# A two-layer squared-ReLU MLP: the first chunk's first layer split into two token halves

## The chip, the cores and the metric

The kernel runs on one core of one Trainium2 chip. Times are device microseconds (us) of a whole execution. A time is about 1.8 us longer than the span that the profile covers (118.68 against 116.9 us in the profiled run). Each timed run also records the mean clock that TensorE was granted. Runs of one kernel are called slow when they are over 1.5% above its fastest run, and the verdicts compare fast runs only. The recorded clock is either 0.999 to 1.0, or 0.985 and, twice, 0.971. I say "full clock" and "dipped" for the two, and compare full-clock runs with full-clock runs.

## The reference

```python
B, S, D, F = 1, 2048, 640, 1536            # all tensors bf16
h = jnp.einsum("bsd,df->bsf", x, w1) + b1
r = jnp.where(h > 0, h, 0)
out = jnp.einsum("bsf,fd->bsd", r * r, w2) + b2
```

## The kernel before

The 2048 tokens are taken in 4 chunks of 512. The first layer makes h with F on the partitions, in 12 F-blocks of 128; each F-block is a sum over KD = 5 blocks of the D dimension. ScalarE (ACT) applies bias and ReLU from PSUM, VectorE (DVE) squares, and the second layer multiplies with w2, 128 tokens by 320 output columns at a time. A layer of one chunk is about 13 us of TensorE time.

The opening is special. Chunk 0 of x is loaded row by row in two halves of 256 tokens and transposed on TensorE. The five D-blocks of w1 arrive one after the other, so the loads are on the clock. The kernel works in rows: one row takes one D-block `k` of w1, for one token half, over the first six F-blocks, which sit in six PSUM banks of 512 columns.

```python
def pass_matmul(j, k, half, last):          # one F-block j, one D-block k, 256 tokens
    reqs = [(s_w1k[k], 16), (s_xT, half * KD + k + 1)]
    ...
    pe.matmul(banks[bname][:, half * HC:(half + 1) * HC],
              lhsT=w1_sb[:, k, j * P:(j + 1) * P], rhs=xT[:, k, half * HC:(half + 1) * HC],
              start=(k == 0 and half == 0), stop=(k == KD - 1), ...)

def pass_row(k, half):
    for j in range(NPASS):                  # NPASS = 6 of the 12 F-blocks
        pass_matmul(j, k, half, False)

dummy(NDUM0)                                # 7 throw-away matmuls while x loads
...                                         # transposes of token half 0
pass_row(0, 0)
pass_row(1, 0)
t_unit(1, 0, ...); t_unit(1, 1, ...)        # transposes of token half 1
pass_row(2, 0)
...                                         # further rows of both halves, k = 4 last
for j in range(NPASS, KF):                  # the other six F-blocks, all 512 tokens
    for k in range(KD):
        mm1_matmul(j, k, ...)
...                                         # then the second layer of chunk 0
```

The loads are issued in this order: x half 0, w1 blocks 0 and 1, x half 1, w1 block 2, b1, w1 blocks 3 and 4, b2, w2.

## Time and profile before

| before | |
|---|---|
| median of the first 4 runs | 117.76 us (116.51 to 118.68) |
| span of the profiled run | 116.9 us |
| TensorE busy | 111.9 us, 96% of the span |
| first matmul of the second layer (in the chain) | 23.56 us |

From the page of the kernel before come the busy times of the engines and two groups: line, engine, operation, out from in, count, busy us and mean ns of one, then idle us before them and what ended it.

```profile
PE 111.9 (96%) x694; PEld 68.0 (58%) x694; DVE 38.7 (33%) x91; ACT 33.8 (29%) x51; POOL 0.7 (1%) x6
L282 PE MATMUL o_ps<-w_sb,r2T 128*128 128x320 bf16 (+1 forms) x396 | 52.8, 295 | 0.0
L245 PE MATMUL h_ps<-xT,w_sb 128*128 128x256 bf16 x30 | 6.0, 323 | 1.8 <-DMA w_sb<-in_w_dram 1.8
```

The whole of TensorE's waiting for data is in line 245, the rows of the opening: 1.8 us for w1. The chain of waits of the same run (start us, us, what) shows how much of the program an opening can move:

```profile
2.69 6.74 DMA w_sb<-in_w_dram
9.42 0.05 issue
9.47 0.82 PE h_ps L245 x3
...
22.48 1.08 PE o_ps L263 x5
23.56 13.04 PE o_ps L282 x96
36.60 12.95 PE h_ps L263 x60
```

The chain runs through the load of the third w1 block, then through TensorE with no further wait. After 23.56 us come pieces of 13.04 and 12.95 us in turn, 96 and 60 matmuls one after the other without a wait. So the date of the first second-layer matmul decides the time. The timeline of TensorE (start us, us, engine, line, operation; in brackets the idle time before and what ended it) shows the two waits, and something else:

```profile
7.65 0.50 PE L245 MATMUL h_ps<-xT,w_sb 128*128 128x256 bf16 x3 [1.30 <-DMA w_sb<-in_w_dram]
9.47 0.82 PE L245 MATMUL h_ps<-xT,w_sb 128*128 128x256 bf16 x3 [0.50 <-DMA w_sb<-in_w_dram]
11.15 0.85 PE L245 MATMUL h_ps<-xT,w_sb 128*128 128x256 bf16 x3
14.31 0.49 PE L245 MATMUL h_ps<-xT,w_sb 128*128 128x256 bf16 x3
```

Three matmuls take 0.50 us at 7.65, over 0.8 us at 9.47 and 11.15, and 0.49 us again at 14.31. The windows view (stretch, its length, then busy us and count of PE, PEld, DVE, ACT and POOL, the granted clock PEclk, DMA share, GB/s) gives the reason:

```profile
6.13:9.54 3.41, 1.50 (x13) 0.82 (x12) 0.49 (x2) 0.00 (x0) 0.00 (x0) 0.99 1.00 356
9.54:12.96 3.42, 3.42 (x20) 2.61 (x21) 0.58 (x3) 0.00 (x0) 0.00 (x0) 0.51 0.86 292
12.96:16.37 3.41, 3.41 (x32) 2.87 (x31) 0.22 (x1) 0.52 (x2) 0.00 (x0) 1.00 0.95 347
```

In a stretch in which TensorE was busy 1.50 of 3.41 us, the clock was still full; in the next stretch of the same length it was halved. The clock records of this trace begin at about 6.1 us: full for 3.413 us, half for 3.413 us, then full for 105.813 us, which is 31.0 times 3.413; in the trace of the changed kernel the full clock lasts 109.226 us, 32.0 times 3.413. So I take stretches of 3.41 us, counted from the first record, as the windows to look at. That the work in one window decides the clock of the next is my reading of the traces. Here the window before the dip was not wholly idle, it was 44% busy. The dip lasts 3.41 us and, at a granted clock of 0.51, costs, by my estimate, about half of that, 1.7 us, of work.

### The profile page before, as it was taken

To read this page: it belongs to the slowest core of one execution; us is meant where nothing else is said; L and a number is where in the kernel's file an instruction comes from. 1 tells how busy PE (TensorE), PEld (TensorE's weight loads), DVE (VectorE), ACT (ScalarE), POOL (GpSimd) and SP (SyncE) were. 2 spreads that over 40 slices of the span, in tenths; PEclk is the share of its full clock that TensorE was granted. 3 is DMA by queue.
4 is the path that set the end of the run, shared out by engine and by line. 5 is a ranking of instruction groups with operands and counts; after the bars stand their busy time and mean duration, and the time that the engine had idled before them with its cause. 6 is when DMAs were issued, how large, how long until landed. Compare 5 with 4: busy or idle time off the path is not lost.

```text
span 116.9 us, 1659 instructions
## 1 busy us (share of the span) xinstructions
PE 111.9 (96%) x694; PEld 68.0 (58%) x694; DVE 38.7 (33%) x91; ACT 33.8 (29%) x51; POOL 0.7 (1%) x6
## 2 busy tenths in 40 slices
PE   7958999999999999999999999999999999999992
PEld 2525784477775444477775444577775444577781
DVE  0303027543323334433322433433332343342331
ACT  5000059720000676520001567610002656700000
POOL 2000000000000000000000000000000000000000
PEclk9996799999999999999999999999999999999999
DMA  3998962701110390001110370001111000001112
GB/s 86 319 340 301 370 217 54 171 0 56 56 41 21 87 193 0 0 0 59 59 59 34 86 161 3 0 0 62 56 56 56 0 0 0 6 0 56 56 56 56
DMA packets 13359, 9.44 MB, mean 81 GB/s; under 512 B 8488, under 2 KB 12712, under 8 KB 13352
## 3 DMA queue, kind: packets, MB, share of 16 engines
q1 hardware_dynamic: 13352, 9.34, 26.4%
q8 instruction: 5, 0.08, 0.3%
q14 instruction: 2, 0.02, 0.0%
HBM read 4.75 MB, written 2.62 MB: 63 GB/s over the span
## 4 chain that ended last, share of the span: by engine, by line
PE 90%; DMA 6%; SPq 1%; issue 0%; DVE 0%
PE o_ps L282 45%; PE h_ps L263 36%; DMA w_sb<-in_w_dram 6%; PE h_ps L245 3%; PE o_ps L245 3%; PE e_ps L263 2%; PE o_ps L263 1%; PE e_ps L233 1%; SPq L181 0%; SPq L182 0%; SPq L184 0%; SPq L183 0%; DVE o_sb L381 0%; PE e_ps L313 0%
## 5 line engine op out<-in xcount | busy, mean ns | idle before, releaser
L282 PE MATMUL o_ps<-w_sb,r2T 128*128 128x320 bf16 (+1 forms) x396 | 52.8, 295 | 0.0
L282 PEld LDWEIGHTS o_ps<-w_sb,r2T 128*128 128x128 bf16 x396 | 38.1, 98 | 14.9
L351 ACT ACTIVATE r_sb<-h_ps,b1T 128x512 bf16<-128x512 f32 x42 | 28.7, 689 | 55.8 <-PE h_ps L263 53.6
L263 PE MATMUL h_ps<-xT,w_sb 128*128 128x512 bf16 x195 | 42.7, 379 | 0.0
L263 PEld LDWEIGHTS h_ps<-xT,w_sb 128*128 128x128 bf16 x195 | 19.1, 98 | 22.5
L372 DVE TENSOR_TENSOR r2T<-r_sb 128x512 bf16<-128x512 bf16 x48 | 20.4, 425 | 32.0 <-ACT r_sb L351 32.0
L381 DVE TENSOR_TENSOR o_sb<-o_ps,b_bc 128x320 bf16<-128x320 f32 (+1 forms) x33 | 15.9, 481 | 33.5 <-PE o_ps L282 33.5
L245 PE MATMUL h_ps<-xT,w_sb 128*128 128x256 bf16 x30 | 6.0, 323 | 1.8 <-DMA w_sb<-in_w_dram 1.8
L245 PE MATMUL o_ps<-xT,w_sb 128*128 128x256 bf16 x30 | 5.7, 312 | 0.0
L245 PEld LDWEIGHTS h_ps<-xT,w_sb 128*128 128x128 bf16 x30 | 3.0, 114 | 2.8 <-DMA w_sb<-in_w_dram 2.3
L365 DVE COPY xT<-e_ps 128x256 bf16<-128x256 bf16 x7 | 1.8, 290 | 6.4 <-PE e_ps L233 6.4
L227 PE MATMUL o_ps<-const-bfloat16-1.0 128*128 128x512 bf16 x7 | 3.1, 624 | 0.8 <-PEq L410 0.8
L245 PEld LDWEIGHTS o_ps<-xT,w_sb 128*128 128x128 bf16 x30 | 3.4, 114 | 0.8
L343 ACT ACTIVATE b1T<-e_ps 128x12 f32<-128x12 bf16 x1 | 0.2, 181 | 11.5 <-PE e_ps L313 11.5
L351 ACT ACTIVATE r_sb<-o_ps,b1T 128x512 bf16<-128x512 f32 x4 | 2.5, 702 | 0.4 <-PE o_ps L263 0.4
L263 PE MATMUL e_ps<-xT,w_sb 128*128 128x512 bf16 x10 | 2.3, 379 | 0.0
L233 PE MATMUL e_ps<-ident,x_sb 128*128 128x128 bf16 x14 | 2.1, 286 | 0.1
L365 DVE COPY xT<-h_ps 128x256 bf16<-128x256 bf16 x3 | 0.7, 292 | 4.4 <-PE h_ps L233 4.4
L227 PEld LDWEIGHTS o_ps<-const-bfloat16-1.0 128*128 128x128 bf16 x7 | 0.9, 135 | 2.1 <-issue 2.1
L233 PEld LDWEIGHTS e_ps<-ident,x_sb 128*128 128x128 bf16 x14 | 1.5, 135 | 0.6 <-issue 0.4
L263 PEld LDWEIGHTS e_ps<-xT,w_sb 128*128 128x128 bf16 x10 | 1.0, 98 | 1.0
L342 ACT ACT_TABLE_LOAD x1 | 1.3, 1283 | 0.7 <-PEq L410 0.7
(14 smaller groups left out, 5.8 us busy)
## 6 DMA issues: line engine op xcount, KB each, us to landing
out_dram<-o_sb SPq DMA_DIRECT2D x15, 160.0 KB, 1.8
w_sb<-in_w_dram SPq DMA_DIRECT2D x5, 384.0 KB, 6.7
w_sb<-in_w_dram SPq DMA_DIRECT2D x1, 1920.0 KB, 12.4
x_sb<-in_x_dram SPq DMA_DIRECT2D x2, 320.0 KB, 4.7
b_bc<-in_b_dram SPq DMA_DIRECT2D x1, 160.0 KB, 7.4
out_dram<-o_sb SPq DMA_DIRECT2D x1, 80.0 KB, 1.6
out_dram<-o_sb SPq DMA_DIRECT2D x2, 40.0 KB, 1.5
xT<-in_x_dram SPq DMA_TRANSPOSE x3, 4.8
```

What stands on the lines that cost most here:

```text
L227: pe.matmul(banks["o0"], lhsT=ones_w, rhs=ones_m, start=True, stop=True)
L233: ins = pw.emit(reqs if q == 0 else [], lambda: pe.transpose(out=stage[(half, k)][:, q * P:(q + 1) * P], in_=x_sb[:, t, k * P:(k + 1) * P] ...
L245: ins = pw.emit(reqs, lambda: pe.matmul(banks[bname][:, half * HC:(half + 1) * HC], lhsT=w1_sb[:, k, j * P:(j + 1) * P], rhs=xT[:, k, half ...
L263: ins = pw.emit(reqs, lambda: pe.matmul(banks[bname], lhsT=w1_sb[:, k, j * P:(j + 1) * P], rhs=xT[:, k, c * CH:(c + 1) * CH], start=(k == ...
L282: ins = pw.emit(reqs, lambda: pe.matmul(banks[bname][:, 0:nc_], lhsT=r2T[:, j, i * P:(i + 1) * P], rhs=w2_sb[:, j, c0:c0 + nc_], start=(j ...
L342: act.activation(out=junk[:, 0:1], in_=zero_c, func=ACT.Relu)
L343: aw.emit([(s_b1ps, 1)], lambda: act.activation(out=b1T[:], in_=e_ps[:, 1, 0:KF], func=ACT.Identity)).then_inc(s_b1T, 1)
L351: aw.emit(reqs, lambda: act.activation(out=r_sb[:, n % NR, :], in_=banks[g1_bank[n]], func=ACT.Relu, bias=b1T[:, j:j + 1], scale=1.0,)).th ...
L365: dw.emit([(s_T, u + 1)], lambda: dve.tensor_copy(out=xT[:, k, half * HC:(half + 1) * HC], in_=stage[(half, k)],)).then_inc(s_xT, 1)
L372: dw.emit([(s_r, n + 1)], lambda: dve.tensor_tensor(out=r2T[:, j, c * CH:(c + 1) * CH], in0=r_sb[:, n % NR, :], in1=r_sb[:, n % NR, :], op ...
L381: dw.emit([(s_b2, 16), (s_o, m + 1)], lambda: dve.tensor_tensor(out=o_sb[:, i, c0:c0 + nc_], in0=banks[g2_bank[m]][:, 0:nc_], in1=b2_bc[:, ...
```

## The change

The intent: do the first layer of chunk 0 for one token half over all 12 F-blocks, then for the other half, so that work downstream (activation, square, second layer of the first 256 tokens) can start earlier.

```diff
-    x_v = x2.rearrange("(i p) d -> p i d", p=P)
+    x_v0 = x2[0:CH, :].rearrange("(p t) d -> p t d", t=TPC)     # 4 neighbouring tokens per partition
+    out_v0 = out2[0:CH, :].rearrange("(p t) d -> p t d", t=TPC)
...
+        for half in range(2):
+            for j in range(KF):
+                q = j // 2                                      # two F-blocks share one bank
+                bname = (pass_banks if half == 0 else b0_banks)[q]
+                G1.append(dict(..., tok0=half * HC, ntok=HC, bank=bname, col0=(j % 2) * HC, ...))
...
-                    reqs = [(s_r2, c * KF + j + 1)]
+                    reqs = [(s_r2, n_of(i, j) + 1)]             # only the half that holds token tile i
...
-            def pass_row(k, half):
-                for j in range(NPASS):
-                    pass_matmul(j, k, half, False)
+            def pass_row(k):
+                for j in range(KF):                             # 12 F-blocks instead of 6
+                    half_matmul(G1[j], k, j % 2 == 0, [])
...
-            pass_row(0, 0)
-            pass_row(1, 0)
+            pass_row(0)
+            pass_row(1)
...                                                             # rows 2 and 3, k = 4, then all of half 1
```

A PSUM bank (a part of 512 columns of the kernel's `psum_tensor` buffers, in which it adds up the five D-blocks of a sum) that held one F-block of 512 tokens now holds two F-blocks of 256 tokens, and only the first of the two starts with `start=True`. All eight experiment runs of kernels built that way are recorded as correct; no run here starts both, so what a second start would do is not shown. The cost of the change is 12 more ACT and 12 more DVE operations, each half as wide, and 120 matmuls of 256 columns where there were 60 of 256 and 30 of 512.

## The prediction

> **What bounds the kernel now.** The page's busy table gives the TensorE 111.9 us of a 116.9 us span (96%), and the chain of waits is 90% TensorE. From 23.56 us on (first second-layer matmul) the chain is TensorE with no gap: alternating pieces of 13.04 and 12.95 us, then 13.09 and a short tail. The change does not touch those 93.3 us. So only the time until the first second-layer matmul can move.
>
> In that opening the timeline shows TensorE waiting 1.3 us for the second block of w1 (6.34 to 7.65 us), and 0.5 us for the third (to 9.47). The rows before use only 6 of the 12 F-blocks per arriving w1 block, so TensorE runs dry. From the issue times and times to landing, I put the fourth and fifth blocks at about 10.5 and 11.4 us, w2 at about 18.2 us. From 9.54 to about 12.95 us the window view gives a granted clock of 0.50: there a 256-column matmul takes 0.213 us instead of 0.109. [...] It costs about 1.7 us, and would explain that the four times fall into 116.5 and 117.0 against 118.6 and 118.7: with or without it.
>
> **What the change does.** Same multiplications: 60 matmuls of 256 plus 30 of 512 columns become 120 of 256. Measured spacing 0.109 against 0.216 us, so +0.06 us. Weight loads are 98 ns and stay hidden. But each arriving w1 block now feeds 12 matmuls at once, so 12 more (1.3 us) are done by the time the third block lands. ACT and DVE get 24 half-size operations instead of 12 in the first chunk: the 512-column ones come every 0.58 us; I estimate 0.36 us for half size, so ACT lags TensorE by up to 3 us but ends near 22 us; the first second-layer groups (6.5 us) need only the first token half, so this is hidden. The x loads get 2560-byte runs: 1280-byte packets take 61 ns, 3072-byte ones 141, so hardly a gain.
>
> **Critical path after** (estimate, full clock): second w1 block 7.65; 12 matmuls 1.31; transposes 0.4; third row 1.31; transposes 0.4; fourth 1.31; 0.3; fifth 1.31; second half 60 x 0.109 = 6.54: second-layer start at about 20.5 us. With full clock I work out 21.85 for the kernel before; so the gain is 1.3 us in like states. The earlier start of downstream work itself gives nothing beyond that: TensorE was already continuous there.
>
> The shorter idle (0.8 us instead of 1.3, plus little) may also avoid the half-clock window; I give this 60 to 65%. Times: the time exceeds the span by 1.8 us, so 20.5 + 93.3 + 1.8 = 115.6 without, 117.3 with a half-clock stretch.
>
> **Predicted:** 115.7 us, range 114.5 to 117.3. Against the fast runs of before (116.7) that is about 1% faster, so the verdict is most likely within 2%: 0.75; faster by over 2%: 0.21; slower: 0.04.
>
> **Right if:** wait for the second block about 0.8 us, for the third under 0.2; second-layer pieces still 13.0 us each; second-layer start at 20.5 us (22.2 with a half-clock stretch); no TensorE wait on ACT or DVE. **Wrong if:** TensorE waits for r2 or a bank at the second layer's start (ACT slower per half than 0.36 us); w1 blocks land later or in another order; the half-clock stretch appears at another place; the 256-column matmuls run at more than 0.11 us.

## The result and the profile after

The changed kernel takes 115.27 us (median of 11 runs, 114.67 to 115.63) against 116.84 us (16 runs, 116.14 to 118.68). The ratio is 0.987, with a 95% interval of 0.984 to 0.990. It is the mean time of the one kernel's fast runs over that of the other's from the same rounds, so not quite the ratio of these medians. By the interval it is a gain of 1.3%. The outputs are right.

From the page of the changed kernel, the engines and the two groups (line 303 was 282, line 267 was 245):

```profile
PE 109.4 (96%) x724; PEld 70.0 (62%) x724; DVE 40.6 (36%) x103; ACT 35.3 (31%) x63; POOL 0.7 (1%) x6
L303 PE MATMUL o_ps<-w_sb,r2T 128*128 128x320 bf16 (+1 forms) x396 | 52.8, 295 | 0.0
L267 PE MATMUL h_ps<-xT,w_sb 128*128 128x256 bf16 x60 | 7.5, 273 | 0.5 <-DMA w_sb<-in_w_dram 0.5
```

The second layer costs what it cost, ACT and DVE gained 1.5 and 1.9 us that nobody waits for, and the rows wait 0.5 us for w1 instead of 1.8. The mean of 273 against 323 ns is the missing half clock: in a trace of the kernel before without it (below) the same group has 273 too. The chain of waits:

```profile
2.59 6.63 DMA w_sb<-in_w_dram
9.22 0.04 issue
9.27 0.83 PE h_ps L267 x6
...
19.38 1.09 PE o_ps L267 x10
20.47 13.04 PE o_ps L303 x96
33.51 12.95 PE h_ps L286 x60
```

The second layer starts at 20.47 us instead of 23.56, and from there on the pieces are the same 13.04 and 12.95 us. The span fell from 116.9 to 113.8 us: the whole difference lies before the second layer. But the profile of before was a dipped run and this one is not, so of these 3.1 us about 1.7 belong to the dip. The waits of TensorE in the changed kernel (who waited for whom: us in total, times, longest) hold a surprise:

```profile
PE e_ps L255 <- DMA x_sb<-in_x_dram: 0.8, 1, 0.8
PE h_ps L267 <- DMA w_sb<-in_w_dram: 0.5, 1, 0.5
```

I had expected 0.8 us of waiting for the second w1 block. It had landed at 5.9 us in this run, so row 1 followed row 0 at once; the 0.8 us went to the second half of x, whose transposes stand next in TensorE's order, and 0.5 us to the third block. Either way TensorE goes on to run dry until the third block, whose row starts at 9.47 us in the first trace and at 9.27 in this one. That block is the gate, and the useful question is how much was done before it opens.

### The profile page after: what moved, and what is told of

Same layout as the page of the kernel before. It is cut to its first block, busy times and chain, and to the rows that moved or that the text cites. A ratio compares the mean times of both kernels' runs of the same rounds, so it can differ in the third digit from the quotient of the medians.

```text
span 113.8 us, 1746 instructions
## 1 busy us (share of the span) xinstructions
PE 109.4 (96%) x724; PEld 70.0 (62%) x724; DVE 40.6 (36%) x103; ACT 35.3 (31%) x63; POOL 0.7 (1%) x6
## 4 chain that ended last, share of the span: by engine, by line
PE 90%; DMA 6%; SPq 1%; DVE 0%; issue 0%
PE o_ps L303 46%; PE h_ps L286 34%; DMA w_sb<-in_w_dram 6%; PE h_ps L267 5%; PE o_ps L267 3%; PE e_ps L267 2%; SPq L206 0%; SPq L205 0%; SPq L204 0%; SPq L203 0%; PE e_ps L255 0%; DVE o_sb L399 0%; PE e_ps L332 0%
## 5 line engine op out<-in xcount | busy, mean ns | idle before, releaser
L369 ACT ACTIVATE r_sb<-h_ps,b1T 128x512 bf16<-128x512 f32 (+1 forms) x48 | 29.5, 652 | 52.8 <-PE h_ps L286 52.7
L286 PE MATMUL h_ps<-xT,w_sb 128*128 128x512 bf16 x180 | 39.3, 379 | 0.0
L390 DVE TENSOR_TENSOR r2T<-r_sb 128x512 bf16<-128x512 bf16 (+1 forms) x60 | 22.3, 372 | 27.8 <-ACT r_sb L369 26.1
L286 PEld LDWEIGHTS h_ps<-xT,w_sb 128*128 128x128 bf16 x180 | 17.6, 98 | 20.7
L267 PE MATMUL h_ps<-xT,w_sb 128*128 128x256 bf16 x60 | 7.5, 273 | 0.5 <-DMA w_sb<-in_w_dram 0.5
L267 PEld LDWEIGHTS h_ps<-xT,w_sb 128*128 128x128 bf16 x60 | 5.6, 98 | 1.3 <-DMA w_sb<-in_w_dram 0.7
L267 PEld LDWEIGHTS o_ps<-xT,w_sb 128*128 128x128 bf16 x40 | 3.9, 98 | 0.5
L369 ACT ACTIVATE r_sb<-o_ps,b1T 128x256 bf16<-128x256 f32 x8 | 3.3, 558 | 0.0
L267 PE MATMUL e_ps<-xT,w_sb 128*128 128x256 bf16 x20 | 2.3, 272 | 0.0
L267 PEld LDWEIGHTS e_ps<-xT,w_sb 128*128 128x128 bf16 x20 | 2.0, 98 | 0.2
L369 ACT ACTIVATE r_sb<-e_ps,b1T 128x256 bf16<-128x256 f32 x4 | 1.7, 571 | 0.0
```

The source lines that it names most:

```text
L267: return pw.emit(reqs, lambda: pe.matmul(g1_view(g), lhsT=w1_sb[:, k, j * P:(j + 1) * P], rhs=xT[:, k, g["tok0"]:g["tok0"] + HC], start=(k ...
L286: ins = pw.emit(reqs, lambda: pe.matmul(g1_view(g), lhsT=w1_sb[:, k, j * P:(j + 1) * P], rhs=xT[:, k, g["tok0"]:g["tok0"] + CH], start=(k ...
L369: aw.emit(reqs, lambda: act.activation(out=r_sb[:, n % NR, 0:g["ntok"]], in_=g1_view(g), func=ACT.Relu, bias=b1T[:, j:j + 1], scale=1.0,)) ...
L390: dw.emit([(s_r, n + 1)], lambda: dve.tensor_tensor(out=r2T[:, j, g["tok0"]:g["tok0"] + g["ntok"]], in0=r_sb[:, n % NR, 0:g["ntok"]], in1= ...
```

## The experiments

All ratios are to fast runs of the kernel before of the same chip, taken beside it. By the 1.5% rule a dipped run can still be called fast; for the token order alone, the rows of 6 and the wait for both halves, which ran on one chip, three of the five fast runs of before were dipped, so there the full-clock means and the traces count for more than the ratio. The theory: in the wait for the loads, rows of 12 F-blocks do 12 matmuls more (1.3 us) before the third w1 block than rows of 6; and because TensorE idles less, the dip disappears. Rivals: the larger x packets bring the loads in earlier; the earlier start downstream is the gain; the runs with a dip have some other cause.

### The kernel before, at full clock

No edit; one look.

> The kernel before, unchanged, once more for its profile. If the run has no half-clock stretch: span about 115 us, second-layer start near 21.85 us (my arithmetic in the prediction, never seen in a trace). If it has one: 23.5 us as before. When the second w1 block lands is the open point: 7.65 us in the first trace of before, 5.93 us in the trace of the changed kernel.

This run took 116.52 us at a clock of 1.0, with a span of 114.7 us. Its chain of waits:

```profile
2.69 6.21 DMA w_sb<-in_w_dram
8.90 0.05 issue
8.95 0.50 PE h_ps L245 x3
...
21.39 13.04 PE o_ps L282 x96
```

Without a dip the kernel before starts its second layer at 21.39 us; I had worked out 21.85. The third w1 block came 0.5 us earlier here than in the first trace, and that is nearly the whole difference. So the fair measure is the distance from the gate to the second layer: 21.39 - 8.95 = 12.44 us before, and 20.47 - 9.27 = 11.20 us after. The gain by this measure is 1.24 us. I use the distance below, as it takes the luck of the loads out.

This trace also suggests why only some runs of one kernel dip. Its windows view, with the windows laid where the trace's clock records put them:

```profile
3.77:7.18 3.41, 1.88 (x20) 1.29 (x20) 1.08 (x5) 0.00 (x0) 0.00 (x0) 1.00 0.93 303
7.18:10.60 3.42, 2.63 (x28) 2.06 (x26) 0.98 (x4) 0.00 (x0) 0.00 (x0) 1.00 0.89 344
```

In the dipped trace the full clock came only at about 6.1 us (three matmuls of its first row still took 0.85 us), so that both waits for w1, 1.30 and 0.50 us, fell into one window, 1.50 us busy. Here it came at 3.77 us, the waits were shared between two windows, 1.88 and 2.63 us busy, and the clock stayed full. So in these traces a window with 1.50 us of work in 3.41 was followed by half the clock and one with 1.88 was not, and where the windows fall differs from run to run: the full clock began at about 6.1, at 3.77 and, in the trace of the changed kernel, at about 4.7 us. This is read from traces; no run here sets where they fall.

### The token order alone

```diff
  (kernel before)
-            sp.dma_start(out=x_sb[:, 0:2, :], in_=x_v[:, 0:2, :])
+            sp.dma_start(out=x_sb[:, 0:2, :], in_=x_v0[:, 0:2, :])
   (and the same for the second half of x and the first four output tiles)
```

> The kernel before with only the change's token order (x and the first outputs four rows apart, 2560-byte x runs). Theory (wider rows fill the wait): no gain, ratio 0.997 to 1.003 to before, because the third w1 block still gates. Rival (the larger x packets let the weights land earlier, and that is the gain): ratio about 0.987, and every w1 block lands over 1 us earlier.

Measured: 1.002, with a wide interval (0.987 to 1.016), since two of its four runs were dipped. Its two full-clock runs mean 116.6 us, as do the two of before (116.6). In its trace, a full-clock run, the third row starts at 9.30 and the second layer at 21.74: a distance of 12.44 us, unchanged. No block landed a microsecond earlier.

### The change without the token order

```diff
  (changed kernel)
-    x_v0 = x2[0:CH, :].rearrange("(p t) d -> p t d", t=TPC)
+    x_v0 = x2[0:CH, :].rearrange("(t p) d -> p t d", p=P)       # out_v0 likewise
```

> The changed kernel with the token order of before (1280-byte x runs). Theory: the layout is not the gain, ratio to before 0.985 to 0.991. Rival (packets): ratio near 1.00, third w1 block landing later by over 1 us.

Measured: 0.989 (0.984 to 0.994), distance 19.99 - 8.79 = 11.20 us. The gain is all there without the new order. With the run before, this rules the packet rival out.

### Rows of 6 and of 8 in the changed kernel

```diff
  (changed kernel, WROW = 6 or 8)
-                for j in range(KF):
+                for j in range(WROW):
                     half_matmul(G1[j], k, j % 2 == 0, [])
...
-            for q in range(KF // 2):
+            for q in range(WROW // 2):
                 half_matmul(G1[2 * q], KD - 1, True, [])
                 pair_done(half_matmul(G1[2 * q + 1], KD - 1, False, []), G1[2 * q + 1])
+            for q in range(WROW // 2, KF // 2):                 # the rest of half 0, k inside
+                for k in range(KD):
+                    half_matmul(G1[2 * q], k, True, [])
+                    ins = half_matmul(G1[2 * q + 1], k, False, [])
+                pair_done(ins, G1[2 * q + 1])
```

Halves, token order, ACT and DVE work all stay as in the change. Only how many F-blocks stand ready per arriving w1 block is put back.

> The changed kernel, but the rows taken per arriving w1 block are 6 blocks wide again; the other 6 of the first token half follow afterwards. Halves, layout, ACT and DVE work all stay as changed. Theory (wider rows fill the wait): 12 matmuls x 0.109 = 1.3 us are lost again, ratio to before 0.998 to 1.003, second-layer start near 21.8 us in a full-clock run, and slow runs with a half-clock stretch come back. Rival (the token halves by themselves let the second layer start earlier): ratio stays 0.987.

> As the rows-of-6 run, but with rows 8 wide: 4 blocks fewer in each of the two rows that precede the third w1 block. Theory (each missing block costs its matmuls): 2 x 4 x 0.109 = 0.87 us over the changed kernel, ratio to before about 0.995 (rows of 6 gave 0.9996, rows of 12 0.987). Rival (a threshold, for instance only the half-clock stretch matters): the same as rows of 12 or of 6.

| rows of | ratio of fast runs (95%) | gate to second layer | full-clock mean | dipped runs |
|---|---|---|---|---|
| 6 | 1.000 (0.988 to 1.011) | 21.80 - 9.19 = 12.61 us | 116.8 us | 1 of 4 |
| 8 | 0.996 (0.992 to 1.000) | 21.33 - 9.26 = 12.07 us | 116.5 us | 1 of 4 |
| 12 (the change, beside the run of 8) | 0.986 (0.983 to 0.989) | 20.43 - 9.23 = 11.20 us | 115.4 us | 0 of 6 |

The gain is gone with rows of 6. The distance for 8 is 0.87 us above that for 12, exactly 2 rows x 4 blocks x 0.109 us, and for 6 it is 1.41, of which 1.3 are the 12 matmuls. The timeline of TensorE in the run with rows of 8 shows the lost time before the gate:

```profile
5.28 0.38 PE L268 MATMUL o_ps<-xT,w_sb 128*128 128x256 bf16 x2
6.20 0.83 PE L268 MATMUL h_ps<-xT,w_sb 128*128 128x256 bf16 x6 [0.54 <-DMA w_sb<-in_w_dram]
8.39 0.38 PE L256 MATMUL e_ps<-ident,x_sb 128*128 128x128 bf16 x4 [1.14 <-DMA x_sb<-in_x_dram]
9.26 0.83 PE L268 MATMUL h_ps<-xT,w_sb 128*128 128x256 bf16 x6 [0.48 <-DMA w_sb<-in_w_dram]
```

It idles 0.54 + 1.14 + 0.48 us. The run of the changed kernel beside it, the control, idles only 0.43 and 0.48 us in this stretch:

```profile
7.00 0.83 PE L267 MATMUL h_ps<-xT,w_sb 128*128 128x256 bf16 x6 [0.43 <-DMA w_sb<-in_w_dram]
9.23 0.83 PE L267 MATMUL h_ps<-xT,w_sb 128*128 128x256 bf16 x6 [0.48 <-DMA w_sb<-in_w_dram]
```

> The changed kernel unchanged, as the control on the same chip for the three beside it. Theory: ratio 0.985 to 0.989 to before's fast runs, granted clock at least 0.999 in every run (no half-clock stretch in 26 runs so far of kernels with rows of 12), while before shows 0.985 in about half of its runs.

It gave 115.43 us median, ratio 0.986, and a clock of at least 0.999 in all six runs, while 5 of the 11 runs of before beside it were dipped.

### The second layer waits for both token halves again

```diff
  (changed kernel)
             if c == 0:
-                return ((i % TPC) // 2) * KF + j
+                return KF + j
```

> The changed kernel, but the second layer of the first chunk waits, F-block by F-block, for the second token half, as the kernel before did. Theory (the dependency on half the tokens hides only a short ACT/DVE tail): at most 0.2 us slower than the changed kernel, since the squares of the second half end at 22.06 us and the matmul that needs the last of them is due at 21.97; ratio to before 0.986 to 0.990. Rival (the earlier downstream start is the gain): ratio back to about 1.00.

Measured: 0.989 (0.980 to 0.997), 115.95 us median, no dipped run. So the named intent of the change, an earlier start downstream, is not where most of the gain comes from. The ratio flatters this kernel, though: its mean, 115.94 us, is only 0.68 us under the two full-clock runs of before beside it (116.62). By its trace the distance from the gate is still 11.20 us (20.74 - 9.54), and what is lost comes after it. The timeline shows what giving it up costs (PEld is TensorE's weight load):

```profile
20.47 1.29 PEld L303 LDWEIGHTS o_ps<-w_sb,r2T 128*128 128x128 bf16 x10
22.00 0.10 PEld L303 LDWEIGHTS o_ps<-w_sb,r2T 128*128 128x128 bf16 x1 [0.24 <-DVE r2T L390]
22.36 3.65 PEld L303 LDWEIGHTS o_ps<-w_sb,r2T 128*128 128x128 bf16 x28 [0.27 <-DVE r2T L390]
```

The last two squares of chunk 0 are late, and the chain of waits now runs through 24 half-size activations. From the start of the second layer to the next first-layer matmul at 34.09 us I get about 13.35 us instead of 13.04 (the start, 20.74, is the first matmul's record, 20.58, plus the 0.16 us by which the chain dates that matmul later in the changed kernel). That is 0.3 us, so about 0.9 of the 1.24 us are kept; I had allowed a loss of 0.2. The halved dependency is therefore not a gain over the kernel before, which never waited there. It covers a cost that the halving itself brings: 24 activations, one every 0.36 us (six of them in 2.30 us, 0.56 us each in itself), instead of 12 every 0.57 us.

### Is it the idle time that brings the dip?

```diff
  (kernel before)
             pass_row(0, 0)
+            pw.wait_all([(s_xT, 5)])
+            for _ in range(8):                                  # into a bank that is free here; thrown away
+                pe.matmul(banks["e1"][:, 0:HC], lhsT=ones_w, rhs=ones_m[:, 0:HC], start=True, stop=True)
             pass_row(1, 0)
```

> The kernel before with 8 throw-away 256-column matmuls between its first and second row, in the wait for the second w1 block. Theory of the clock: they keep TensorE active, so no half-clock stretch in the profile and no slow runs (before: 4 of 16 over 117.5 us), while its fast runs keep the fast time of before within 0.3%, since nothing useful is done in the gap. Rival (the slow runs come from something else): slow runs in about one of four as before.

> The filled kernel once more, only to count. So far the granted clock was 0.985 or lower in 15 of 30 timed runs of the kernel before, and in 0 of 6 of the filled one. Theory of the clock: again none at 0.985 in the filled kernel, while before shows it in about half; fast times equal within 0.3%. Rival (chance): about half of these runs show it too.

Measured: 1.000 (0.997 to 1.003) the first time and 1.003 (0.998 to 1.007) the second. The filler wins nothing in itself, as it should be: nothing useful is done in the gap. The dips: none of 6, then 1 of 6. The second expectation ("none") was missed by that one run, at 117.9 us. Taken together, 1 of 12 filled runs dipped, against 10 of 24 runs of the kernel before on the same two chips (15 of 31 with the third chip, which had no filled run). If both had the same chance, a split this uneven or more so in this direction would come up in about 4% of cases (counting the ways to place 11 dips among 36 runs). Other runs with the idle time left in (the token order alone, rows of 6 and of 8, and the look at the unchanged kernel) dipped in 4 of 13 cases; and none of the 44 runs listed for kernels with rows of 12 dipped. The traces that record the clock agree: with the filler the least busy window of the opening held 2.52 and 2.32 us of work, with rows of 12 at least 2.25. What these counts don't prove is that nothing else brings a dip.

A dipped run of the kernel before took 118.2 us in the mean on one chip and 118.3 on the other two, against 116.6 to 116.8 at full clock, so a dip costs 1.4 to 1.6 us. On the chip of the control, the mean over all runs was 117.46 us before and 115.39 after: 2.07 us, of which 1.45 remain at full clock (116.84 against 115.39) and 0.62 is the vanished dips.

### Going further: the second half of x after the weights

The changed kernel still waits for the second x half and the third w1 block, and it does not need that x half until all of token half 0 is done.

```diff
  (changed kernel)
-            sp.dma_start(out=x_sb[:, 2:4, :], ...)              # stood between w1 blocks 1 and 2
...
+            sp.dma_start(out=x_sb[:, 2:4, :], ...)              # now after w1 block 4
...
             pass_row(0); pass_row(1); pass_row(2); pass_row(3)  # transposes no longer between them
             for q in range(KF // 2):                            # k = 4
                 ...
+                if q >= 1:
+                    t_unit(1, q - 1, ...)
```

> The changed kernel with the second half of x loaded after the w1 blocks instead of between the second and the third, and its transposes moved behind the fourth row, between the pairs of the fifth. Theory (the third w1 block, at 9.29 us, gates everything after it; the load ahead of it is not needed until then): third, fourth and fifth w1 blocks about 0.9 us earlier, second-layer start 19.2 to 19.8 us, ratio to before 0.976 to 0.982. Rival (bandwidth is shared among all loads, so their order matters little): third block still near 9.3 us and ratio 0.987. If the start moves before 18.3 us plus latency, w2 would be the new limit.

> The same kernel as the run with the second half of x last, for its spread: its spans ran from 112.8 to 113.9 us. Theory: it no longer waits for loads, so TensorE's cold clock in the first row shows in the time (up to 12 x 0.104 = 1.2 us when the clock is released only after the first row); in the trace the span follows the spacing of the first 12 matmuls. Rival: the load order gives nothing and its fast run was chance: ratio to before equal to the control's within 0.1%.

The loads moved as hoped: in the first trace the third block landed 3.51 us after the first x half instead of 5.65 in the changed kernel, and the second layer started at 19.52 us with a span of 112.8 us. But the time did not follow: 115.27 us median and 0.987 the first time, 115.47 and 0.986 the second, when the changed kernel itself had 115.43 and 0.986. Both expectations of a gain were missed; the second time it was the rival's number, the same ratio as the control within 0.1%, that came out. The new order of the loads did take effect, though, so the question is what gates instead. TensorE's timeline of the second trace answers it:

```profile
7.33 0.83 PE L267 MATMUL h_ps<-xT,w_sb 128*128 128x256 bf16 x6 [1.22 <-DMA w_sb<-in_w_dram]
13.93 2.36 PE L267 MATMUL e_ps<-xT,w_sb 128*128 128x256 bf16 x20 [0.39 <-DVE xT L381]
```

Now the second w1 block gates. It landed 2.5 us after the first x half in the fast trace and 3.7 us after it in this one, though the first w1 block came at 0.93 and 0.94 us in both. My theory that a slow first row makes the spread is not supported by this trace: its first row ran at full speed (6 matmuls in 0.81 us) and its span was the long one, 114.0 us. There is also a 0.39 us wait for the last transposed copy, which I removed next:

```diff
  (the kernel with the second half of x last)
-        b0_banks = ["e0", "e1", "h0", "h1", "h2", "o0"]
+        b0_banks = ["h0", "h1", "h2", "o0", "e0", "e1"]
```

> The same, and the second half's first groups take the banks h0, h1, h2, o0, with e0 and e1, where the transposes are staged, last. It should remove the 0.39 us that TensorE waited for the last transposed copy: 0.3 to 0.4 us less than its neighbour, span 112.5 to 113.5 us, ratio to before 0.979 to 0.984, under the changed kernel by 0.5 to 1.0 us. If nothing changes, the wait only moved to the last k step of the first group.

The wait is gone: in its trace TensorE waits for no data at all. The median is 115.00 us, ratio 0.984 (0.980 to 0.988), and the mean is 0.25 us under that of the control beside it, with overlapping intervals. That is under what I expected (0.5 to 1.0 us). In its trace the first row began at about half speed:

```profile
4.78 1.49 PE L267 MATMUL h_ps<-xT,w_sb 128*128 128x256 bf16 x6
6.06 0.93 PE L267 MATMUL o_ps<-xT,w_sb 128*128 128x256 bf16 x6
6.83 0.82 PE L267 MATMUL h_ps<-xT,w_sb 128*128 128x256 bf16 x6
```

The first six take 1.49 us instead of 0.82. In this kernel that slow start is no longer hidden in a wait. So this version is the lowest of those measured, but not by an amount that six runs prove. What limits it is not settled: its own trace shows the slow start of the first row, 1.49 us instead of 0.82, and a trace of the kernel it was made from shows a wait of 1.22 us for the second w1 block.

## Why the prediction was right

The time, 115.27 us, lies in the range of 114.5 to 117.3 and near the 115.7 predicted. Point by point:

- **Only the opening can move.** Right: the pieces after the second layer's start are 13.04 and 12.95 us in both traces.
- **12 more matmuls before the gate, 1.3 us.** Right: the distance from the third w1 block to the second layer fell from 12.44 to 11.20 us, by 1.24. Rows of 8 and 6 give back 0.87 and 1.41 us. At full clock the timed runs of one chip differ by 1.45 us; I put the 0.2 above the 1.24 down to when the loads land, which I did not show.
- **Second layer at 20.5 us without a dip.** Right: 20.47. The date rests on a compensation: the prediction let the second block gate at 7.65 us, which put the third row at 9.36; in fact the second x half and the third block held TensorE up, and the third row started at 9.27. That the two agree is luck.
- **Waits of 0.8 us for the second and under 0.2 for the third block.** Wrong in detail: none for the second, 0.8 for the second x half, 0.5 for the third; in the control's trace 0.43 for the second and 0.48 for the third. I had read one landing time from one trace as if it were fixed. In the traces of all kernels the second block lands 1.95 to 4.0 us after the first x half.
- **A chance of 60 to 65% that the dip goes.** Too low: none of the changed kernel's 18 listed runs dipped (12 where its median counts 11, and 6 of the control). The filler experiment ties the dip to the idle time, but not perfectly: 1 of 12 against 10 of 24. The reason given, the shorter idle, left out how the idle time falls across two windows: of the two traces of before, the one that dipped had 1.50 us of work in its least busy window, the other 1.88.
- **ACT at 0.36 us per half-size operation, hidden.** Right: 0.36 us, ending at 21.7 us, with no wait of TensorE on ACT or DVE.
- **"The earlier start of downstream work itself gives nothing."** Nearly right: without it the changed kernel would lose 0.3 of its 1.24 us, but only because the change made ACT's tail longer.
- **The x layout hardly matters.** Right: a distance of 12.44 us with it alone, 11.20 us without it.

## What to carry to other kernels

While loads arrive piece by piece, the time is set by how much work each piece unlocks (rows of 6, 8 and 12 gave 12.61, 12.07 and 11.20 us from the gate to the second layer): find the load that gates, count the matmuls that could be done before it lands, and give the engine those. Judge such a change by the distance from the gate to the next stage, in runs of one clock state, because the landing times wander: the third block's by 0.75 us over the eleven traces with this order of loads, the second's, counted from the first x half, by 2.1 us over all traces, against an effect of 1.24. A short wait can also go with a cost beyond itself: here waits of 1.30 and 0.50 us were followed by 3.42 us at a granted clock of 0.51, and a dipped run was 1.4 to 1.6 us longer; that part shows only in the average over all runs. And an earlier load need not shorten the whole: with the second half of x last, the third block landed 2.0 and 0.8 us earlier than in the two traces of the changed kernel, and the median stayed where it was.

## Two more measurements

- In the first layer of the later chunks 60 matmuls of 512 columns, each with its weight load of 98 ns, take 12.95 us, 216 ns each, in every chunk; in the rows at full clock 6 matmuls of 256 columns take 0.66 us in the chain of waits, 109 ns each.
- The sixteen parts of one load land far apart: in the first trace of before, those of the second w1 block landed between 1.55 and 3.71 us after the first x half, twelve of them by 2.25, and the row that waited for the block began at 7.65 us, 0.04 us after the last part. A 3072-byte packet took 0.12 us in the median there, and single ones up to 1.1 us; in the trace of the changed kernel a single 2560-byte packet took 1.67 us. What delays them is open.
